# Query transposes a step ahead, and a new order of loads and TensorE work at the start, in a fused retention and feed-forward kernel

## The chip, the cores and the metric

The kernel runs on one core of a Trainium2 chip. The metric is the device time of one execution in microseconds (us). A profile is one further look at an execution; its span is some 2 us shorter than the device time, because the program's ends are not in it. All runs told of are of the fast state unless said otherwise. "Step" is the work on 256 tokens (there are twelve, 0 to 11); the steps 0 to 2 are written out ahead of the main loop, which runs from 3 to 11. At the undisturbed pace a step of the loop takes 12.18 us.

## The reference

```python
# retention: per head h a 64x64 state that decays by gamma[h] at every token
for t in range(S):                                    # S = 768, 4 batches, 8 heads, D = 64
    state = gamma * state + outer(k[:, :, t], v[:, :, t])
    y[:, :, t] = scale * q[:, :, t] @ state
x = y as rows of [B*S, H*D]                           # 3072 x 512
# feed-forward without activation
a = x @ w1; b = x @ w2                                # 512 -> 1024
out = (a * b) @ w3 @ w_out                            # w3 @ w_out is multiplied once, in the kernel
```

The kernel computes the recurrence in chunks of 64 tokens: scores of queries with keys inside a chunk, masked; their product with the scaled values ("attention" below); and a running state from keys and values, whose product with the queries is added. Queries and keys must be transposed for that. In the loop the DMA engine does it.

## The kernel before

Everything below is issued in program order on each engine: there is no scheduler between. All DMAs, loads, stores and transposes, are issued by SyncE, in this order. Cuts are marked.

```python
    w3_st = {f: load_rows(moe_w3, f) for f in range(4, 8)}
    load_q(0); load_q(1)
    load_k(0); load_v(0)
    w1_st = [load_rows(moe_w1, d) for d in range(4)]
    load_k(1); load_v(1)
    w2_st = [load_rows(moe_w2, d) for d in range(4)]
    # ... q2, q3, then keys, values and queries of the steps 2 to 4

    def q_dma(n):                 # transpose of one query tile, issued on SyncE
        qT = att.tile([128, 2, NP, 128], HP, tag="qT", name="qT", bufs=5)
        nc.sync.dma_start_transpose(qT..., q16s.pop(n)[:, :])       # cut

    def step(m):
        inter(m - 1)              # state products of the step before
        outputs_back(m - 1, 0); outputs_back(m - 1, 1)              # VectorE
        am_back = scores(m)       # needs the keys of m and BOTH query tiles of the pair
        am_back(0); am_back(1)
        if m > 5:
            q_dma(m + 2)
        ffn[m - 2].o_unit(0)      # 8 output products, eviction on ScalarE, store
        k_cast(m + 1, (nc.scalar,)); k_dma(m + 1)
        ffn[m - 2].o_unit(1)
        load_k(m + 2); load_v(m + 2)
        load_q(m + 3 if m < 6 else m + 4)
        for f in range(2):
            ffn[m - 1].ab(f)      # a- and b-products; ScalarE and VectorE evict
        if m == 5:
            q_cast(7, nc.scalar); q_dma(7); load_q(9)
        intra(m)                  # attention
        # ... kv, state updates, ab(2), ab(3)
        v_cast(m + 1, (nc.gpsimd, nc.gpsimd))
        if m == 4:
            q_cast(6, nc.gpsimd); q_dma(6)
        elif m > 4:
            q_cast(m + 3, nc.gpsimd)
        for f in range(4, 8):
            ffn[m - 1].ab(f)
```

Two query tiles serve two steps: 6 and 7 for the steps 6 and 7. Both are needed when step 6's scores begin.

Of the kernel before, what the change touches and what calls it, by code (L numbers as in the profile page):

```python
# [18 lines left out]
def kernel(  # L19
# [11 lines left out]
    nc = tc.nc  # L31
# [47 lines left out]
    def load_k(m):  # L79
        load_kv(m, k_in, k)  # L80

    def load_v(m):
        load_kv(m, v_in, v)
# [41 lines left out]
    w3_st = {f: load_rows(moe_w3, f) for f in range(4, 8)}  # L125
    load_q(0)
    load_q(1)
    load_k(0)
    load_v(0)
    w1_st = [load_rows(moe_w1, d) for d in range(4)]  # L130
    load_k(1)
    load_v(1)
    w2_st = [load_rows(moe_w2, d) for d in range(4)]
    load_q(2)
    load_q(3)
# [56 lines left out]
    def cast_to(dst, src, on_dve):  # L192
        if on_dve:
            nc.vector.tensor_copy(dst, src)
        else:
            nc.scalar.copy(dst, src)  # L196
# [78 lines left out]
    def k_cast(m, engs):  # L275
        k16 = att.tile([128, 2, 512], HP, tag="k16", name="k16", bufs=3)
        k32 = k_in.pop(m)
        if len(engs) == 1:
            parts = [(k16[:, :, :].rearrange("p e x -> p (e x)"), k32[:, :, :].rearrange("p e x -> p (e x)"))]
        else:  # L280
            parts = [(k16[:, e, :], k32[:, e, :]) for e in range(2)]
        for eng, (dst, src) in zip(engs, parts):
            (nc.scalar.copy if eng is nc.scalar else eng.tensor_copy)(dst, src)  # L283
        k16s[m] = k16

    def v_cast(m, engs):
        v16 = att.tile([128, 2, 512], HP, tag="v16", name="v16", bufs=3)
        v32 = v_in.pop(m)
        for e, eng in enumerate(engs):
            eng.tensor_tensor(  # L290
                v16[:, e, :].rearrange("j (h d) -> j h d", d=D),
                v32[:, e, :].rearrange("j (h d) -> j h d", d=D),
                VS[:, :].unsqueeze(2).broadcast_to((128, H, D)),
                MULT,
            )
        v16s[m] = v16
# [25 lines left out]
    def k_transposes(m, tag, on_dve):  # L322
        k16, kT = k16s[m], new_kT(m)
        if tag:
            ps = bank(tag, [128, 2, NP, 128], HP, "psTk")
        else:
            ps = ps_f.tile([128, 2, NP, 128], HP, tag="psF", name="psTk")
        for e in range(2):
            for p in range(NP):
                nc.tensor.transpose(ps[:, e, p, :], k16[:, e, p * 128 : (p + 1) * 128], ident16[:, :])  # L330
        for e in range(2):
            cast_to(kT[:, e, :, :], ps[:, e, :, :], on_dve[e])
# [17 lines left out]
    def scores(m, engs=None):  # L350
        kT = kTs.pop(m)
        am = att.tile([128, 2, NP * 2, L], HP, tag="am", name="am")
        ps = [bank(f"X{r}", [128, NP * 2, L], FP, "psA") for r in range(2)]
        for e in range(2):
            for p in range(NP):
                for r in range(2):
                    for s in range(2):
                        nc.tensor.matmul(  # L358
                            ps[r][half(s), p * 2 + e, :], lhsT=kT[half(r), e, p, half(s)],
                            rhs=queries(m, e, p, s, r), start=True, stop=True,  # L360
                        )
        AMs[m] = am

        def back(r):
            nc.vector.tensor_tensor(  # L365
                am[:, r, :, :], ps[r][:, :, :],
                keep[:, :].unsqueeze(1).broadcast_to((128, NP * 2, L)), MULT,
            )

        return back  # L370
# [52 lines left out]
    def inter(m):  # L423
        ps = psYs[m]
        t = [Ts[m, s] for s in range(2)]
        first = t[0] is None
        for e in range(2):
            for p in range(NP):
                u = p * 2 + e
                for s, r in ((1, 0), (1, 1)) if first else ((1, 0), (0, 1), (0, 0), (1, 1)):  # L430
                    nc.tensor.matmul(  # L431
                        ps[s][half(r), u, :], lhsT=t[s][half(r), u * L : (u + 1) * L],
                        rhs=queries(m, e, p, s, r), start=False, stop=(e == 1 and p == NP - 1),
                    )

    def outputs_back(m, s):
        if m not in XT:
            XT[m] = xpool.tile([128, NP * 2, 2, L], HP, tag="xt", name="xt")
        order = "p u (t i) -> p u t i"
        nc.vector.tensor_tensor(  # L440
            XT[m][:, :, s, :].rearrange("p u (i t) -> p u t i", t=2),
            psYs[m][s][:, :, :].rearrange(order, t=2),
            YS[:, :, :].rearrange("p a (e x) -> p (a e) x", e=2).rearrange(order, t=2), MULT,
        )
# [52 lines left out]
    def cast_w(W, st, d, on_dve):  # L497
        cast_to(W[d][:, :], st[d][:, :], on_dve)

    def busy(m, tag="Y0"):  # L500
        ps = bank(tag, [128, 512], FP, "psZ")
        for _ in range(m):
            nc.tensor.matmul(ps[:, :], lhsT=Z[:, 0:128], rhs=Z[:, 0:512], start=True, stop=True)  # L503
# [30 lines left out]
    k_transposes(0, "X0", (True, False))  # L534
    w3o_back()
    v_cast(0, (nc.gpsimd, nc.vector))
    nc.gpsimd.tensor_copy(W1[1][:, :], w1_st[1][:, :])
    cast_w(W1, w1_st, 0, False)
    backs = []

    def first_scores():
        backs.append(scores(0))

    w3o_back = w3_mm(7, first_scores)
    w3o_back()
    backs[0](0)
    backs[0](1)
    intra(0)
    backs.append(kv(0, True))
    busy(3, "X0")  # L550
    backs[1](0)
    inter(0)
    busy(3, "X1")
    outputs_back(0, 0)
    outputs_back(0, 1)
    backs[1](1)
    cast_w(W1, w1_st, 2, False)
    cast_w(W1, w1_st, 3, False)

    ffn = [Ffn(m) for m in range(NSTEP)]  # L560
    f0, f1 = ffn[0], ffn[1]
# [3 lines left out]
    def four_banks():  # L565
        return [ps_f.tile([128, 2, TB], FP, tag="psF", name="psF")[:, :, :] for _ in range(4)]

    def by_rows(W, ps, d, blocks=range(8)):
        for f in blocks:
            nc.tensor.matmul(  # L570
                ps[f // 2][:, f % 2, :], lhsT=W[d][:, f * 128 : (f + 1) * 128],
                rhs=f0.x(d), start=(d == 0 and f % 2 == 0), stop=(d == 3 and f % 2 == 1),
            )

    k_cast(1, (nc.gpsimd, nc.scalar))
    ps = four_banks()
    by_rows(W1, ps, 0)
    by_rows(W1, ps, 1)
    by_rows(W1, ps, 2)
    k_transposes(1, "Y0", (True, False))  # L580
    by_rows(W1, ps, 3, range(4))
    pa = [hold[i // 2][:, i % 2 * 512 : i % 2 * 512 + 512].rearrange("p (a n) -> p a n", a=2) for i in range(4)]
    am_back = scores(1)
    by_rows(W1, ps, 3, range(4, 8))
    for i in range(4):
        cast_to(pa[i], ps[i], False)
    am_back(0)
    am_back(1)
    v_cast(1, (nc.gpsimd, nc.gpsimd))
    nc.gpsimd.tensor_copy(W2[0][:, :], w2_st[0][:, :])  # L590
    ps = four_banks()
    cast_w(W2, w2_st, 1, False)
    intra(1)
    kv_back = kv(1)
    kv_back(0, nc.vector)
    by_rows(W2, ps, 0)
    inter(1)
    outputs_back(1, 1)
    outputs_back(1, 0)
    cast_w(W2, w2_st, 2, False)  # L600
    nc.gpsimd.tensor_copy(W2[3][:, 512:1024], w2_st[3][:, 512:1024])
    q_cast(2, nc.gpsimd)
    kv_back(1)
    by_rows(W2, ps, 1)
    nc.scalar.copy(W2[3][:, 0:512], w2_st[3][:, 0:512])
    by_rows(W2, ps, 2)
    f1.a_unit(0, "X0")
    by_rows(W2, ps, 3)
    for i in range(4):
        nc.vector.tensor_tensor(f0.HT[:, 2 * i : 2 * i + 2, :], pa[i], ps[i], MULT)  # L610
    q_cast(3, nc.gpsimd)
    for f, tag in ((1, "Y1"), (2, "Y0"), (3, "X1"), (4, "X0"), (5, "Y1"), (6, "Y0"), (7, "X1")):
        f1.a_unit(f, tag)
    k_cast(2, (nc.gpsimd, nc.scalar))
    q_transposes(2, "X0", True)
    f0.o_unit(0)
# [27 lines left out]
    def step(m):  # L644

        inter(m - 1)
        outputs_back(m - 1, 0)
        outputs_back(m - 1, 1)
        if m >= NSTEP:
            return  # L650
        am_back = scores(m)
        am_back(0)
        am_back(1)
        if m > 5:
            q_dma(m + 2)
        ffn[m - 2].o_unit(0)
        if m + 1 < NSTEP:
            k_cast(m + 1, (nc.scalar,))
            k_dma(m + 1)
        ffn[m - 2].o_unit(1)  # L660
        load_k(m + 2)
        load_v(m + 2)
        load_q(m + 3 if m < 6 else m + 4)
        for f in range(2):
            ffn[m - 1].ab(f)
        if m == 5:
            q_cast(7, nc.scalar)
            q_dma(7)
            load_q(9)
        intra(m)  # L670
        kv_back = kv(m)
        kv_back(0)
        ffn[m - 1].ab(2)
        ffn[m - 1].ab(3)
        kv_back(1)
        if m + 1 < NSTEP:
            v_cast(m + 1, (nc.gpsimd, nc.gpsimd))
        if m == 4:
            q_cast(6, nc.gpsimd)
            q_dma(6)  # L680
        elif m > 4:
            q_cast(m + 3, nc.gpsimd)
        for f in range(4, 8):
            ffn[m - 1].ab(f)
# [42 lines left out]
```

## Time and profile before

| | before |
|---|---|
| device time, median of 3 | 198.76 us (197.88 to 199.11) |
| span of the profile | 196.1 us |
| TensorE busy | 180.8 us, 92% |
| granted clock, mean | 0.983 |

The busy share reads as if TensorE were the bound everywhere. It is, in the steps; but one wait stands out in the list of what TensorE's matmuls waited for (total us, how often, the longest):

```profile
PE psA L358 <- DMA qT<-q: 5.2, 1, 5.2
```

One wait, once: 5.2 us for a query transpose. The next longest waits in that list are of 1.3 and 1.1 us, at the start of the program and at the second step's keys.

### The profile page before, as it was taken

The numbers are of one execution on the slowest core, as the hardware profiler recorded it, in microseconds if no ns is written. First come the engines' busy times: TensorE is split into PE (matmuls) and PEld (weight loads), VectorE is DVE, ScalarE is ACT, GpSimd is POOL, SyncE is SP. The second block draws the span as 40 slices with busy tenths as digits, with TensorE's granted clock in tenths as the row PEclk, the third lists the DMA queues.
The fourth block names the chain that finished last, engine by engine and source line by source line (L and its number), as shares of the span: only waits on it lengthen the run. The fifth ranks groups of instructions, "written<-read, shape, count | busy, mean of one in ns | idle before, by whom it ended". The sixth has DMA issues, their size and how long they took to land.

```text
span 196.1 us, 6231 instructions
## 1 busy us (share of the span) xinstructions
PE 180.8 (92%) x2651; PEld 126.8 (65%) x2651; DVE 96.7 (49%) x187; ACT 87.5 (45%) x165; POOL 64.1 (33%) x92
## 2 busy tenths in 40 slices
PE   7799998679998999999908999999999999999993
PEld 2355655558675785877803685877858678586772
DVE  1226356068378255674432265664556735555240
ACT  5578545475553544327400544325443264232432
POOL 6200233536618071280601044280732607120000
PEclk9999999999999999999995899999999999999999
DMA  6999999999999999999998696989969550110202
GB/s 213 370 390 384 255 278 344 270 357 250 231 220 238 253 205 234 226 244 215 258 229 154 166 233 162 243 206 187 207 162 215 116 160 3 57 53 3 107 0 107
DMA packets 87338, 40.23 MB, mean 205 GB/s; under 512 B 67728, under 2 KB 82320, under 8 KB 87312
## 3 DMA queue, kind: packets, MB, share of 16 engines
q1 hardware_dynamic: 87312, 39.85, 84.0%
q8 instruction: 20, 0.33, 0.7%
q14 instruction: 6, 0.05, 0.1%
HBM read 29.36 MB, written 6.29 MB: 182 GB/s over the span
## 4 chain that ended last, share of the span: by engine, by line
PE 68%; SPq 12%; DMA 11%; DVE 4%; ACT 1%; issue 1%; DVEq 0%; ACTq 0%
PE psF L460 33%; PE psO L485 23%; SPq L60 12%; DMA stg<-in_moe_w_out_dram 4%; DMA stg<-in_k_dram 4%; DMA qT<-q 3%; PE psY L431 3%; PE psA L358 2%; PE psG L460 2%; PE psY L380 2%; PE psF L570 1%; DVE ht L475 1%; PE psK L400 1%; DVE am L365 1%; PE psTk L330 1%
## 5 line engine op out<-in xcount | busy, mean ns | idle before, releaser
L460 PE MATMUL psF<-xt,w 128*128 128x256 f16 x672 | 77.1, 273 | 0.0
L460 PEld LDWEIGHTS <-w 128*128 128x128 f16 x704 | 68.0, 98 | 10.3
L475 DVE TENSOR_TENSOR ht<-pa,psF 128x256 f16<-128x256 f32 x88 | 36.6, 420 | 54.3 <-ACT pa L469 29.7
L418 POOL TENSOR_TENSOR t<-s,GS 128x512 f16<-128x512 f32 x19 | 24.1, 1267 | 71.8 <-DVE s L417 71.8
L469 ACT COPY pa<-psF 128x256 f32<-128x256 f32 x80 | 29.7, 371 | 39.9 <-PE psF L460 39.9
L485 PE MATMUL psO<-w3o,ht 128*128 128x512 f16 (+2 forms) x200 | 46.2, 386 | 0.0
L485 PEld LDWEIGHTS <-ht 128*128 128x128 f16 x200 | 19.2, 101 | 21.5 <-issue 3.3
L489 ACT ACTIVATE osb<-psO 128x512 f32<-128x512 f32 (+2 forms) x25 | 14.5, 580 | 40.0 <-PE psO L485 40.0
L290 POOL TENSOR_TENSOR v<-stg,VS 128x512 f16<-128x512 f32 x23 | 23.5, 1042 | 5.5 <-DMA stg<-in_v_dram 3.9
L365 DVE TENSOR_TENSOR am<-psA,keep 128x512 f16<-128x512 f32 x24 | 15.3, 679 | 7.0 <-PE psA L358 7.0
L440 DVE TENSOR_TENSOR xt<-psY,YS 128x512 f16<-128x512 f32 x24 | 16.1, 722 | 1.7 <-PE psY L431 0.8
L269 POOL CAST q<-stg 128x1024 f16<-128x1024 f32 x8 | 8.3, 1036 | 23.6 <-DMA stg<-in_q_dram 23.6
L417 DVE TENSOR_TENSOR s<-psK,t 128x512 f32<-128x512 f32 x20 | 13.8, 688 | 3.4 <-PE psK L400 2.7
L283 ACT CAST k<-stg 128x1024 f16<-128x1024 f32 (+1 forms) x12 | 11.2, 934 | 5.1 <-DMA stg<-in_k_dram 4.9
L358 PE MATMUL psA<-qT,kT 64*64 64x64 f16 x384 | 6.6, 197 | 6.6 <-DMA qT<-q 5.2
L215 DVE COPY w3t<-psW 128x1024 f16<-128x1024 f16 x8 | 5.4, 689 | 11.7 <-PE psW L223 9.2
L358 PEld LDWEIGHTS <-kT 64*64 64x64 f16 x384 | 5.1, 108 | 8.1 <-issue 5.9
L196 ACT CAST w3h<-stg 128x1024 f16<-128x1024 f32 x8 | 8.3, 1043 | 3.6 <-DMA stg<-in_moe_w_dram 3.5
L431 PEld LDWEIGHTS <-t 64*64 64x64 f16 x352 | 6.5, 109 | 3.6 <-issue 2.1
L503 PE MATMUL psZ<-zeros 128*128 128x512 f16 x19 | 7.6, 553 | 1.3 <-DVE zeros L142 1.3
L431 PE MATMUL psY<-qT,t 64*64 64x64 f16 x352 | 7.8, 194 | 0.7 <-DVE t L418 0.6
L244 PE MATMUL psW<-wo,w3t 128*128 128x512 f16 x32 | 8.4, 399 | 0.0
(58 smaller groups left out, 121.2 us busy)
## 6 DMA issues: line engine op xcount, KB each, us to landing
stg<-in_moe_w_dram SPq DMA_DIRECT2D x16, 512.0 KB, 6.6
stg<-in_q_dram SPq DMA_DIRECT2D x12, 512.0 KB, 6.9
stg<-in_k_dram SPq DMA_DIRECT2D x24, 256.0 KB, 5.4
stg<-in_v_dram SPq DMA_DIRECT2D x24, 256.0 KB, 5.2
out_dram<-osb SPq DMA_DIRECT2D x23, 256.0 KB, 2.5
stg<-in_moe_w_out_dram SPq DMA_DIRECT2D x4, 512.0 KB, 7.8
out_dram<-osb SPq DMA_DIRECT2D x1, 160.0 KB, 1.8
qT<-q SPq DMA_TRANSPOSE x8, 4.0
```

The source lines that it names most:

```text
L60: nc.sync.dma_start(dst, src)
L290: eng.tensor_tensor(v16[:, e, :].rearrange("j (h d) -> j h d", d=D), v32[:, e, :].rearrange("j (h d) -> j h d", d=D), VS[:, :].unsqueeze(2 ...
L358: nc.tensor.matmul(ps[r][half(s), p * 2 + e, :], lhsT=kT[half(r), e, p, half(s)], rhs=queries(m, e, p, s, r), start=True, stop=True,)
L365: nc.vector.tensor_tensor(am[:, r, :, :], ps[r][:, :, :], keep[:, :].unsqueeze(1).broadcast_to((128, NP * 2, L)), MULT,)
L418: eng.tensor_tensor(t16[:, :], s32[:, :], gs, MULT)
L431: nc.tensor.matmul(ps[s][half(r), u, :], lhsT=t[s][half(r), u * L : (u + 1) * L], rhs=queries(m, e, p, s, r), start=False, stop=(e == 1 an ...
L440: nc.vector.tensor_tensor(XT[m][:, :, s, :].rearrange("p u (i t) -> p u t i", t=2), psYs[m][s][:, :, :].rearrange(order, t=2), YS[:, :, :] ...
L460: nc.tensor.matmul(ps[:, :], lhsT=W[d][:, f * 128 : (f + 1) * 128], rhs=self.x(d), start=(d == 0), stop=(d == 3),)
L469: nc.scalar.copy(self.pa[f][:, :], ps[:, :])
L475: nc.vector.tensor_tensor(self.HT[:, f, :], self.pa.pop(f)[:, :], ps[:, :], MULT)
L485: nc.tensor.matmul(psO[:, :], lhsT=self.HT[:, f, e * 128 : (e + 1) * 128], rhs=W3O[f][:, cs], start=(f == 0), stop=(f == 7),)
L489: nc.scalar.activation(osb[:, cs], psO[:, :], AF.Copy, scale=final_scale)
```

## The change

Its intent: (1) take the late query transpose out of the loop's way, by casting both tiles of a pair in one place and issuing both transposes at the head of the step before they are needed (query 7 is cast at the end of step 4 instead of in the middle of step 5; query 6's transpose moves from the end of step 4 to the head of step 5); (2) in the start-up, load the second step's keys and values ahead of w1, compute its attention early, and have the a-products of the second step fill the time in which w2's rows come in.

```diff
     load_q(1)
-    load_k(0)
-    load_v(0)
+    for m in range(2):
+        load_k(m)
+        load_v(m)
     w1_st = [load_rows(moe_w1, d) for d in range(4)]
-    load_k(1)
-    load_v(1)
     w2_st = [load_rows(moe_w2, d) for d in range(4)]
@@ start-up, attention of step 0
-    nc.gpsimd.tensor_copy(W1[1][:, :], w1_st[1][:, :])
-    cast_w(W1, w1_st, 0, False)
+    k_cast(1, (nc.gpsimd, nc.scalar))
     ...
     backs.append(kv(0, True))
-    busy(3, "X0")                      # filler matmuls
     backs[1](0)
+    k_transposes(1, "X0", (False, False))
+    w3o_back()
     inter(0)
-    busy(3, "X1")
     outputs_back(0, 0)
     outputs_back(0, 1)
     backs[1](1)                        # state update, GpSimd
-    cast_w(W1, w1_st, 2, False)
-    cast_w(W1, w1_st, 3, False)
+    v_cast(1, (nc.gpsimd, nc.gpsimd))  # values of step 1, GpSimd
+    nc.gpsimd.tensor_copy(W1[1][:, :], w1_st[1][:, :])
+    for d in (0, 2, 3):
+        cast_w(W1, w1_st, d, False)
@@ attention of step 1, W1's and W2's rows (before: W1's rows, keys, scores, W2's rows and attention in turn)
+    busy(2, "X1")
     am_back = scores(1)
     am_back(0)
     am_back(1)
     intra(1)
     kv_back = kv(1)
     kv_back(0, nc.vector)
+    by_rows(W1, ps, 0)
     inter(1)
     ...
+    by_rows(W1, ps, 1)  ...  by_rows(W1, ps, 3)
+    f1.a_unit(f, tag)                  # f = 0..3
     by_rows(W2, ps, 0)
+    f1.a_unit(f, tag)                  # f = 4..7
     by_rows(W2, ps, 1)  ...  by_rows(W2, ps, 3)
-    f1.a_unit(f, tag)                  # f = 1..7, after w2's last row
@@ loop
-        if m > 5:
+        if m > 3 and m % 2:
+            q_dma(m + 1)
             q_dma(m + 2)
     ...
+        load_q(m + 3) if m % 2 == 0 else None
         load_k(m + 2)
         load_v(m + 2)
-        load_q(m + 3 if m < 6 else m + 4)
+        load_q(m + 3) if m % 2 else None
     ...
-        if m == 5:
-            q_cast(7, nc.scalar)
-            q_dma(7)
-            load_q(9)
     ...
-        if m == 4:
-            q_cast(6, nc.gpsimd)
-            q_dma(6)
-        elif m > 4:
+        if m % 2 == 0:
+            q_cast(m + 2, nc.gpsimd)
             q_cast(m + 3, nc.gpsimd)
```

(The second and third blocks are cut to their core and partly put in order for reading; the loop's are whole.)

More of the change, by code (lines that the diff above doesn't have):

```diff
@@ L544 @@
     w3o_back = w3_mm(7, first_scores)
-    w3o_back()
     backs[0](0)
@@ L573, in by_rows @@
             )
-    k_cast(1, (nc.gpsimd, nc.scalar))
-    ps = four_banks()
-    by_rows(W1, ps, 0)
-    by_rows(W1, ps, 1)
-    by_rows(W1, ps, 2)
-    k_transposes(1, "Y0", (True, False))
-    by_rows(W1, ps, 3, range(4))
     pa = [hold[i // 2][:, i % 2 * 512 : i % 2 * 512 + 512].rearrange("p (a n) -> p a n", a=2) for i in range(4)]
+    busy(2, "X1")
     am_back = scores(1)
-    by_rows(W1, ps, 3, range(4, 8))
-    for i in range(4):
-        cast_to(pa[i], ps[i], False)
     am_back(0)
     am_back(1)
-    v_cast(1, (nc.gpsimd, nc.gpsimd))
-    nc.gpsimd.tensor_copy(W2[0][:, :], w2_st[0][:, :])
-    ps = four_banks()
-    cast_w(W2, w2_st, 1, False)
     intra(1)
@@ L595 @@
     kv_back(0, nc.vector)
-    by_rows(W2, ps, 0)
+    ps = four_banks()
+    by_rows(W1, ps, 0)
     inter(1)
@@ L599 @@
     outputs_back(1, 0)
+    by_rows(W1, ps, 1)
+    kv_back(1)
+    nc.gpsimd.tensor_copy(W2[0][:, :], w2_st[0][:, :])
+    by_rows(W1, ps, 2)
+    by_rows(W1, ps, 3)
+    for i in range(4):
+        cast_to(pa[i], ps[i], i % 2 == 1)
+    cast_w(W2, w2_st, 1, False)
+    for f, tag in ((0, "X0"), (1, "Y1"), (2, "Y0"), (3, "X1")):
+        f1.a_unit(f, tag)
+    ps = four_banks()
+    by_rows(W2, ps, 0)
     cast_w(W2, w2_st, 2, False)
+    for f, tag in ((4, "X0"), (5, "Y1"), (6, "Y0"), (7, "X1")):
+        f1.a_unit(f, tag)
+    by_rows(W2, ps, 1)
+    nc.scalar.copy(W2[3][:, 0:512], w2_st[3][:, 0:512])
     nc.gpsimd.tensor_copy(W2[3][:, 512:1024], w2_st[3][:, 512:1024])
     q_cast(2, nc.gpsimd)
-    kv_back(1)
-    by_rows(W2, ps, 1)
-    nc.scalar.copy(W2[3][:, 0:512], w2_st[3][:, 0:512])
     by_rows(W2, ps, 2)
-    f1.a_unit(0, "X0")
     by_rows(W2, ps, 3)
@@ L611 @@
     q_cast(3, nc.gpsimd)
-    for f, tag in ((1, "Y1"), (2, "Y0"), (3, "X1"), (4, "X0"), (5, "Y1"), (6, "Y0"), (7, "X1")):
-        f1.a_unit(f, tag)
     k_cast(2, (nc.gpsimd, nc.scalar))
```

## The prediction

> **What bounds the kernel now.** I read the page's busy shares first, then the slices of TensorE, its clock and the DMA, then the chain of waits, then TensorE's waits, and last the timeline where the chain leaves TensorE.
>
> ```profile
> span 196.1 us, 6231 instructions
> PE 180.8 (92%) x2651; PEld 126.8 (65%) x2651; DVE 96.7 (49%) x187; ACT 87.5 (45%) x165; POOL 64.1 (33%) x92
> ...
> PE   7799998679998999999908999999999999999993
> ...
> PEclk9999999999999999999995899999999999999999
> DMA  6999999999999999999998696989969550110202
> ```
>
> TensorE is busy 92% of the span, no other engine half of it. Its row has two weak places: slices 7 to 9 (about 34 to 49 us, the start-up) and a zero at slice 20 (98 to 103 us), directly followed by the only two slices with a low clock. The DMA row is full to about 98 us, so the start-up is fed at the rate of the loads.
>
> The chain of waits, in order of time, around that zero:
>
> ```profile
> 97.19 1.02 SPq L60
> 98.21 0.05 issue
> 98.26 0.02 SPq L313
> 98.28 0.03 issue
> 98.31 5.24 DMA qT<-q
> 103.54 0.04 issue
> 103.59 0.43 PE psA L358 x12
> 104.02 6.03 PE psO L485 x16
> 110.05 1.75 PE psF L460 x16
> ```
>
> The scores of step 6 wait for a transpose of queries. It could only be issued at 98.31, because SyncE issues in order and was busy up to then with the loads of step 5. It lands 5.24 us later. The 16 output products after it take 6.03 us; in every other step the same entry reads 3.56. TensorE's clock, stretch by stretch:
>
> ```profile
> 98.00:100.00 2.00, 0.43 (x36) 0.34 (x29) 1.53 (x3) 0.00 (x0) 0.00 (x0) 1.00 0.82 182
> 100.00:102.00 2.00, 0.00 (x0) 0.00 (x0) 0.00 (x0) 0.00 (x0) 0.00 (x0) 1.00 1.18 280
> 102.00:103.00 1.00, 0.00 (x0) 0.00 (x0) 0.00 (x0) 0.00 (x0) 0.25 (x1) 0.58 1.09 223
> 103.00:104.00 1.00, 0.41 (x17) 0.35 (x17) 0.00 (x0) 0.00 (x0) 0.79 (x1) 0.50 1.15 294
> ```
>
> (After the bounds and length stand the busy times of PE, PEld, DVE, ACT and POOL, then granted clock, DMA share, GB/s.) After some 4 us of idleness the clock falls to a half; it stays there to about 109 us.
>
> In the start-up the chain runs through a load, the second step's keys:
>
> ```profile
> 28.07 8.59 DMA stg<-in_k_dram
> 36.66 0.02 issue
> 36.68 0.63 ACT k L283
> 37.31 0.05 issue
> 37.35 0.41 PE psTk L330 x4
> ```
>
> **What the Trainium skill says.** (1) "TensorE: Matmul & The Clock Gate", section "Why this matters for your kernels": keep TensorE's idle gaps under about 3 us, or one idle window puts it back to half clock. The trace agrees: 5.2 us of idleness cost the clock, the start-up's gaps (longest 1.1 us in the waits) did not. (2) "Perfetto Trace Analysis", section "DMA Instruction — HWDGE (DVE, Sync)": the profiled span of a DMA instruction is the issuing sequencer's part; the data movement is not in it. Here too: that transpose has a span of 2.36 us on SyncE but lands 5.24 us after its start. (3) "DMA: Bandwidth & Descriptors", section "Why small descriptors are slow (HBM only)": a 256-byte descriptor carries a fixed overhead. The keys and values are such rows (64 floats). The trace agrees: the casts that wait for loads start at 30.05, 31.33, 32.58 and 34.00 for the four w1 rows of 512 KB (1.3 us apart), then 35.18 and 36.68 for two halves of the keys of 256 KB (1.5 us apart), so about half the rate.
>
> **Part 1: query transposes a step ahead.** Now the transpose for query 7 is issued in the middle of step 5, behind five loads; after the change both casts (queries 6 and 7) run on GpSimd at the end of step 4, and both transposes head the SyncE queue of step 5, ahead of its stores, key transpose and loads. Nothing is added: as many transposes as before, and one query cast moves from ScalarE to GpSimd (1.04 us each on either). GpSimd has room: it is busy 4.5 us of the 12.18 us of step 4.
>
> What it takes away: from the start of step 5's outputs (86.33) to that of step 7's (118.30) the kernel needs 31.97 us, and two undisturbed steps need 2 × 12.18 = 24.36. Excess: 7.6 us, of which 5.2 are the wait and 2.5 the half clock (6.03 − 3.56). All of it lies on the path.
>
> Is the new place early enough? GpSimd finishes the values of step 5 at 86.56 and casts query 6 by 87.55, as before. Query 7's load now goes ahead of keys and values in step 4, so issue near 81 to 82, and with the 6.9 us that such loads take it has landed by 89; cast by 90. SyncE: transpose 6 at 87.57 (2.48 us), transpose 7 at about 90.05 (1.2 to 2.5 us), a store, then the key transpose of step 6 at about 92.5 to 93.2 instead of 90.78. Key transposes land 3.0 to 5.7 us after issue, median 3.4: 96 to 98.5. Needed at 98.1. So it is just in time; I charge 0.5 us. The loads of step 6 and 7's keys slip by about 2.5 us with it, but keys are cast on ScalarE some 9 us before their scores. In later steps the DMA share falls (0.84 in the step from 118.30), so the pairs of transposes cost nothing there.
>
> **Part 2: the start-up.** The bytes up to w2's end are the same, so w2's last row still lands at 44.3. Only the order changes. I shift landings by the gaps seen: keys 1 at about 29.7 and 31.0, values 1 at 32.3 and 33.4, w1's rows at 35.0, 36.3, 37.6, 38.9. Filler matmuls fall from 6 to 2: 4 × 0.27 = 1.1 us of TensorE work less.
>
> TensorE then, with durations from the timeline: transposes of keys 1 end near 32.1 (the ScalarE half waits for the load), the first step's state products near 32.55, filler, scores of step 1 at 33.5 to 33.95 (after two ScalarE evictions of 0.58). Next it needs step 1's scaled values. They stand on GpSimd behind the state update, which waits for VectorE's outputs (32.4 to 33.75) and sum (0.69): update 34.5 to 35.75 (1.27), values 36.8 and 37.8 (2 × 1.04). So TensorE is nearly idle from 33.95 to 37.8, but for 0.2 us at 36.9. Then: 0.8 us of attention, W1's first row, 0.6 us waiting for the state, W1's other rows (0.87 each) to 43.25. Here f1's a-products (8 × 0.436 = 3.5) and W2's rows (4 × 0.87 = 3.5) follow almost without gaps, with ScalarE nearly full (four casts or halves, eight copies of 0.37, two evictions): W2's last row ends near 50.7, not 46.6, but with the a-products done. Two query transposes, the key transpose and both outputs, partly behind four VectorE products of 0.69: scores of step 2 near 55.9, against 54.51. So a loss of 1.3 us. Of it about 0.4 comes back at step 3's keys: before, TensorE waited 0.38 us for that cast. Net +0.9: the a-products come forward in the order, but the hole in front of step 1's attention, 3.9 us, is larger than the idleness that they fill. Since orders like this are usually tuned on a chip and my landing times may be off by a microsecond, I count +0.6, and add 0.3 for the chance (one in eight) that the hole costs the clock for some 2.5 us.
>
> **Sum.** 198.76 − 7.6 + 0.5 + 0.9 = 192.56, say 192.6 us (ratio 0.969).
>
> **The rivals.** (a) *The wait moves to the key transpose.* SyncE stays in order and now has three transposes in a row in step 5. For it: transposes and loads in the stretch 86 to 98 us run at a DMA share of 1.20, and the chain of waits before 98 us is already all SyncE. Against it: 0 to 2 us of slack by the sum above. If it is late by 2 us (no clock loss), the time is 194.1. (b) *The start-up gains.* If keys land earlier or GpSimd keeps values ahead, the a-products before w2 save up to the 3.1 us that they take after w2's last row now: 189 us. Against it: TensorE's work is the same but for 1.1 us, and step 3's keys were cast at 57.86 only on landing, with the DMA full, so it can't run far ahead. (c) *The hole before step 1's attention costs the clock.* Idle 3.9 us with a blip of 0.2, close to the 4 us after which it fell at 102; then some 2.5 us more: 195. (d) *The DMA loses its pause.* In the wait it caught up; without it, step 6's keys and values may be late. Against it: a steady step from 118.30 moves 193 GB/s, and 233 to 236 were moved in steps 4 and 5.
>
> **Range and chances.** The wait's removal is sure to about 0.7 us as far as it goes; (a) takes up to 2, the start-up lies between −2.5 and +3. Low 189.5, high 195.8. The limit for 2% is 194.8; (a) and (c) together or a bad start-up reach it: faster 0.81, within 2% 0.17, slower 0.02.
>
> **What would show it.** Right: TensorE's row without a zero and its clock without a low slice after 98 us; steps 5 and 6 of 12.2 us; no wait for a query transpose over 0.5 us; both transposes issued between 87 and 93 us. Start-up: a gap of TensorE of 3 to 4 us at about 34 to 38, ended by GpSimd's values; step 2's scores at about 56. Wrong: a wait of scores for a key transpose of over 1 us in step 6; a half clock at 38 to 44; or step 2's scores before 54, which would mean that the landing times or GpSimd's order were misjudged.

## The result, and the profile after

| | before | after |
|---|---|---|
| device time, median of fast runs | 198.76 us (3 runs) | 192.12 us (191.48 to 193.78, 4 runs) |
| ratio | | 0.9687, interval 0.9598 to 0.9777: faster |
| span of the profile | 196.1 us | 192.1 us |

Ratios here are the mean time of one kernel's fast runs over that of the other's of the same rounds, as the record gives them, so not quite the ratio of the medians. Redone from the single times, some of them leave out a profiled execution; that moves them by 0.001 or less, but for the one told of in experiment 10. A later run of the kernel before in the changed kernel's rounds took 202.87 us and is left out as slow. The profiled execution after the change was its slowest, 193.78 us, and that of before one of its fastest, 197.82: two spans alone would understate the gain. The result is correct in all runs told of here.

The page after the change, the lines that answer to those of before:

```profile
span 192.1 us, 6226 instructions
PE 179.4 (93%) x2647; PEld 126.9 (66%) x2647; DVE 97.4 (51%) x188; ACT 84.7 (44%) x163; POOL 65.0 (34%) x93
...
PE   7799988299999799999999998999999999999993
...
PEclk9999999859999999999999999999999999999999
DMA  5999999999999799999999998999989960110202
```

Two readings. The zero at slice 20 is gone, and so is the low clock behind it. But there is a new low place: slice 7 of TensorE, 34 to 38 us, is down to 2, and in this slice and the next the clock is at 8 and 5 tenths. The chain of waits through the loop, where the stall was (start, duration, what):

```profile
100.47 0.56 PE psY L430 x28
101.08 0.27 PE psA L357 x26
101.36 3.56 PE psO L484 x16
```

Step 6's scores follow at once on step 5's state products, and its 16 output products take 3.56 us, where before stood a wait of 5.24 and products of 6.03. A few lines further down the same chain has something that was not in the kernel before:

```profile
109.61 7.66 DMA stg<-in_k_dram
...
118.29 0.60 ACT osb L488
118.93 0.60 PE psF L459 x4
```

Keys for step 8 take 7.66 us from their issue to landing; ScalarE waits for them with an output's eviction queued behind; the matmuls, out of free accumulators, wait 0.8 us for this eviction. The same chain (keys, ScalarE, eviction, matmuls) stands there once more at 142 us, with hardly any wait of the matmuls.

The new hole in the start-up, on TensorE's timeline (start, duration, instruction, and in brackets the idle time before it and who ended it):

```profile
33.35 0.56 PE L357 MATMUL psA<-qT,kT 64*64 64x64 f16 x32
36.61 0.33 PE L379 MATMUL psY<-am,v 64*64 64x64 f16 x16 [2.70 <-POOL v L289]
37.61 0.43 PE L379 MATMUL psY<-am,v 64*64 64x64 f16 x16 [0.67 <-POOL v L289]
...
38.40 1.89 PE L569 MATMUL psF<-xt,w 128*128 128x256 f16 x8
```

and GpSimd's at the same time:

```profile
34.30 1.26 POOL L417 TENSOR_TENSOR t<-s,GS 128x512 f16<-128x512 f32 x1 [3.70 <-DVE s L416]
35.52 2.04 POOL L289 TENSOR_TENSOR v<-stg,VS 128x512 f16<-128x512 f32 x2
```

The eight matmuls of W1's first row take 1.89 us; at full clock they take 1.05 (experiment 3). What they waited for are step 1's values, which GpSimd scales only after the state update.

To compare starts I use two marks in each profile's chain and timeline, which are free of how fast the very first loads came: the first scores (step 0) and the first of step 3's output products; and as a third the first output products behind the loop.

| profile | first scores | outputs of step 3 | first outputs behind the loop | start-up part | loop part |
|---|---|---|---|---|---|
| before | 28.37 | 62.04 | 179.09 | 33.67 | 117.05 |
| after | 28.84 | 64.82 | 175.06 | 35.98 | 110.24 |

So in this pair the loop gained 6.81 us, the start-up lost 2.31, and the first scores came 0.47 later: 4.0 us together, the difference of the spans. These are one profile each; further profiles below show that the start-up part of one and the same order varies by up to 2 us between profiles.

### The profile page after: what moved, and what is told of

It is laid out like the page before. It is cut to its first block, busy times and chain, and to the rows that moved or that the text cites. A ratio compares the mean times of both kernels' runs of the same rounds, so it can differ in the third digit from the quotient of the medians.

```text
span 192.1 us, 6226 instructions
## 1 busy us (share of the span) xinstructions
PE 179.4 (93%) x2647; PEld 126.9 (66%) x2647; DVE 97.4 (51%) x188; ACT 84.7 (44%) x163; POOL 65.0 (34%) x93
## 4 chain that ended last, share of the span: by engine, by line
PE 65%; DMA 15%; SPq 11%; issue 4%; POOL 2%; ACT 2%; DVE 0%; ACTq 0%; DVEq 0%; POOLq 0%
PE psF L459 32%; PE psO L484 19%; DMA stg<-in_k_dram 10%; SPq L60 9%; PE psF L569 5%; DMA stg<-in_moe_w_out_dram 4%; PE psY L430 3%; PE psG L459 2%; PE psY L379 2%; PE psA L357 1%; PE psK L399 1%; POOL v L289 1%; SPq L489 1%; ACT osb L488 1%; POOL t L417 1%
## 5 line engine op out<-in xcount | busy, mean ns | idle before, releaser
L459 PE MATMUL psF<-xt,w 128*128 128x256 f16 x672 | 77.4, 273 | 0.8 <-ACT osb L488 0.8
L484 PE MATMUL psO<-w3o,ht 128*128 128x512 f16 (+2 forms) x200 | 44.1, 371 | 0.0
L484 PEld LDWEIGHTS <-ht 128*128 128x128 f16 x200 | 18.3, 98 | 20.3 <-DVE ht L609 1.4
L268 POOL CAST q<-stg 128x1024 f16<-128x1024 f32 x9 | 9.2, 1041 | 17.3 <-DMA stg<-in_q_dram 17.3
L569 PE MATMUL psF<-xt,w 128*128 128x256 f16 x64 | 9.7, 317 | 0.0
L379 PE MATMUL psY<-am,v 64*64 64x64 f16 x384 | 5.8, 197 | 3.8 <-POOL v L289 3.4
L379 PEld LDWEIGHTS <-v 64*64 64x64 f16 x384 | 4.4, 110 | 6.6 <-POOL v L289 3.6
```

The source lines that it names most:

```text
L459: nc.tensor.matmul(ps[:, :], lhsT=W[d][:, f * 128 : (f + 1) * 128], rhs=self.x(d), start=(d == 0), stop=(d == 3),)
L484: nc.tensor.matmul(psO[:, :], lhsT=self.HT[:, f, e * 128 : (e + 1) * 128], rhs=W3O[f][:, cs], start=(f == 0), stop=(f == 7),)
L569: nc.tensor.matmul(ps[f // 2][:, f % 2, :], lhsT=W[d][:, f * 128 : (f + 1) * 128], rhs=f0.x(d), start=(d == 0 and f % 2 == 0), stop=(d == ...
```

## The experiments

### 1 and 2. Each part alone

`q_ahead_only` is the kernel before with the loop of the changed one, and nothing else of it; `startup_only` is the changed kernel with the loop of the one before. Their edits are the blocks of the diff above, from "loop" on or up to it.

> The kernel before with the query part of the change alone (casts and transposes of queries a step ahead, load order of queries in the loop); the start-up stays as it was. Theory A (the query part brings all of the gain, the start-up part costs 2.8 us): no wait for a query transpose and no low clock at 98 to 109 us, 190 to 191.5 us, so faster than the whole change (192.1); step 2's scores at 54.5 us as before; 0.5 to 2 us may come back as late keys, for TensorE reaches the loop 2.8 us sooner at the same loads. Rival B (the start-up part helps too, its late end in the one profiled run is chance): slower than the whole change, 193 us or more.

Measured: 191.60 us, ratio 0.9641 (0.9580 to 0.9702), so at least as fast as the whole change. Start-up part 34.20 us, loop part 109.16 (63.70 to 172.86): 7.89 us less than before. Its clock row, from its page:

```profile
PEclk9999999999999999999999999999999999999999
```

> The kernel before with the start-up part of the change alone (keys and values of step 1 ahead of w1, new order); the query transposes stay as they were. Theory A: step 2's scores near 57.4 us instead of 54.5 and a half clock at about 37 to 43 us; the wait in step 6 stays, perhaps some 1 us shorter, because the loop starts later against the same loads; 200 to 202 us. Rival B: under 198 us, and no half clock in the start-up.

Measured: 199.22 us, ratio 1.001 (0.9966 to 1.0055): the same time as before. That is less than theory A's 200 to 202, and more than rival B's 198. Its profile has both losses:

```profile
PEclk9999999879999999999995899999999999999999
```

The clock is low once in the start-up (slices 7 and 8) and once behind the wait in step 6, which stands as it stood:

```profile
100.62 5.14 DMA qT<-q
...
105.81 0.43 PE psA L357 x11
```

Start-up part 34.76 us, 1.1 us longer than before; loop part 116.55, half a microsecond shorter. What follows: the query part brings all of the gain. (It changes the casts, the place of issue and the order of the query loads together; no run takes these apart.) The start-up part brings none, and its order does cost a hole and the clock, but the time it costs is smaller than theory A took from the first pair of profiles.

### 3. Filler matmuls in the hole

```diff
     am_back(0)
     am_back(1)
+    busy(12)
     intra(1)
```

> The kernel after with 12 filler matmuls (12 x 0.216 = 2.6 us) on TensorE between step 1's scores and its attention, where it idles for 2.7 us waiting for GpSimd's values. If the half clock from 37 to 43 us comes from that idleness: clock full throughout, the state products and W1's rows at their usual durations, start-up 2 to 3 us shorter, 189.5 to 190.5 us. If the low clock has another cause (or the hole alone, not the clock, costs the time): 191.5 to 193 us, clock still low there.

Measured: 192.42 us, ratio 0.9668 (0.9617 to 0.9720). The cause of the low clock is confirmed, the price is not. The granted clock was 1.0 in all four executions, against 0.980 to 0.991 in the ten timed runs of the unedited change, here and in later rounds. W1's first row was back at 1.05 us. The fillers delay nothing: step 1's attention begins 7.77 us after the first scores in both profiles. The start-up part was 34.03 us, against 35.98 in the change's first profile and 34.81 in its second (below). But the mean of the timed runs is 192.26 us, with the unedited change at 192.38 in other rounds: a full clock in the start-up was worth nothing that these runs can resolve, where 2 to 3 us were expected. The time expectation failed.

### 4. The values first on GpSimd

```diff
-    backs[1](1)
     v_cast(1, (nc.gpsimd, nc.gpsimd))
+    backs[1](1)
```

> The kernel after with GpSimd's two value products of step 1 moved ahead of its state update of step 0 (1.26 us), which nothing needs before 38 us. Theory A (the hole is GpSimd's order): the wait for values falls from 3.4 us to under 1.5, TensorE starts step 1's attention at about 35 instead of 36.6, the clock stays full, step 2's scores come at 53.5 to 55 instead of 57.4, time 188.5 to 190. Rival C (the values' landing, not GpSimd, is what ends the hole): GpSimd waits for the loads instead, the hole stays over 2.5 us, time 191.5 or more.

Measured: 191.28 us, ratio 0.9621 (0.9565 to 0.9677). The hole is GpSimd's order, not the values' landing: GpSimd starts them at 32.40, and TensorE's attention of step 1 begins at 34.82, held by VectorE's masks, no longer by the values:

```profile
32.40 2.04 POOL L289 TENSOR_TENSOR v<-stg,VS 128x512 f16<-128x512 f32 x2 [1.82 <-DVE t L413]
...
34.82 0.19 PE L379 MATMUL psY<-am,v 64*64 64x64 f16 x1 [0.96 <-DVE am L364]
```

Step 2's scores come at 53.94 (57.30 in the unedited change's profile, 54.51 before): the start-up part is 32.67 us, the shortest so far. Yet 191.28 us lies above the 188.5 to 190 that I expected, and the clock stayed full in the profiled execution only (0.998): the other three had 0.989, 0.980 and 0.981. The profile shows a further loss, in the loop: its steps 3 and 4 took 12.85 and 12.49 us instead of 12.18. Its chain in step 4:

```profile
73.06 4.58 DMA stg<-in_k_dram
...
78.69 0.60 ACT osb L488
79.33 0.60 PE psF L459 x4
```

Keys hold ScalarE, an eviction waits behind them, the matmuls wait for the eviction. My reading is that the loads are further behind the sooner TensorE arrives in the loop; that is argued. The loop part is 110.13 us, one microsecond over the shortest.

### 5 and 6. The change and its query part once more, in the same rounds

> The changed kernel, unedited, so that it stands in the same rounds as the query part alone. Theory A': the start-up part costs 0.4 us for its order and 0.7 to 2 us for the half clock, which comes in every run but ends sooner or later; so 0.5 to 2 us slower than the query part alone, ratio to before 0.966 to 0.972. Rival B': the start-up part is neutral in the timed runs and the two profiles' difference is the loads' chance: within 0.5 us of it. In its profile: half clock from about 37 us; scores of step 0 to outputs of step 3 34.5 to 36 us.

> The query part alone once more. Theory A': 190.5 to 191.5 us, ratio 0.960 to 0.965, clock full or nearly so, scores of step 0 to outputs of step 3 33.5 to 34.3 us as in the kernel before. Rival B': ratio equal to that of the unedited change within 0.003.

Measured: the change 192.17 us, ratio 0.9662 (0.9606 to 0.9717); the query part alone 191.52 us, ratio 0.9618 (0.9566 to 0.9671). Means of six runs each: 192.39 and 191.73. Earlier, each in its own rounds, the means were 192.38 and 191.71. So the start-up part costs about 0.7 us of the whole, twice by the same amount, which is inside what theory A' forecast (0.5 to 2 us), though the intervals of the ratios overlap; it is not settled that it costs anything, but a gain is unlikely. Nor was the query part's clock full throughout: it was 0.982 to 1.0 in these six runs. The second profile of the change has a start-up part of 34.81 us and a loop part of 109.16, without the late keys' stalls of TensorE; the second profile of the query part 34.24 and 109.93, with one of 0.7 us. So late keys come in some executions of either kernel and not in others.

### 7. The clock behind the wait

To weigh the clock alone, the kernel before gets filler matmuls in the place where it waits:

```diff
+        if m == 6:
+            busy(24, "X0")
         am_back = scores(m)
```

> The kernel before with 24 filler matmuls (24 x 0.216 = 5.2 us) on TensorE ahead of step 6's scores, where it waits 5.2 us for the query transpose. If the 6.03 us of the outputs after the wait come from a clock lost to idleness: clock full there, outputs at 3.56 us, the wait itself unchanged, so 2.0 to 2.5 us faster than before (ratio 0.988 to 0.990). If they have another cause (the DMA's catching up, the evictions): outputs still over 5 us, ratio 0.997 to 1.003.

Measured: 197.51 us, ratio 0.9908 (0.9857 to 0.9960); the means of the fast runs are 197.51 and 199.31 (nine of the 11 runs of the kernel before; two are slow): about 1.8 us, with an interval of some 0.8 to 2.9, just under the forecast. The chain at the same place:

```profile
100.47 5.94 DMA qT<-q
...
106.45 0.32 PE psA L358 x16
106.77 3.56 PE psO L485 x16
```

The outputs behind the transpose take 3.56 us again, 2.47 less than before. The transpose is no earlier: in this profile it takes 5.94 us to land instead of 5.24, so that 0.7 us of the gain is lost again. So of what the query part removes, about 2 us were the clock that the wait cost, and the rest the wait. This run taught something else. Its start-up is that of the kernel before, and its clock row reads

```profile
PEclk9999999958999999999999999999999999999999
```

The low slices are 8 and 9, 39 to 49 us: the old start-up loses the clock too, in some executions. In this kernel's six runs the mean clock was 0.982 or 0.983 three times, 0.991 once and 1.0 twice; in the 11 runs of the unedited kernel before in these rounds it lay between 0.966 and 0.991.

### 8. Three more edits on top of the values first

```diff
     by_rows(W1, ps, 0)
+    by_rows(W1, ps, 1)
     inter(1)
     ...
-    by_rows(W1, ps, 1)
@@ step 2
-        k_transposes(3, None, (True, False))
+        k_transposes(3, None, (False, False))
@@ loads
+    load_k(5)                 # after the loads of step 4, before the loop
-        load_k(m + 2)
+        load_k(m + 3)
```

> The changed kernel with the values first on GpSimd and three further edits: W1's second row ahead of step 1's state products (TensorE waited 1.0 us there), both evictions of step 3's transposed keys on ScalarE (scores waited 1.1 us behind VectorE's queue), and each step's keys loaded one step earlier (late keys cost 0.8 to 1.0 us in two profiles). Expected: scores of step 0 to outputs of step 3 about 31 us (32.7 with the values first alone), first to last outputs of the loop 109.1 us, no wait for keys; 188.5 to 190 us, ratio 0.950 to 0.956. If the loads bound the start-up by then: 31.5 us or more there, 190 to 191 us; if the extra early keys push other loads late: a wait for values or a query transpose in steps 3 to 5.

Measured: 192.75 us, ratio 0.9686 (0.9625 to 0.9746): a failure, by its mean 1.8 us slower than the values first alone (193.08 and 191.32, of different rounds; the intervals of the ratios overlap). Start-up part 34.45, loop part 111.37. The clock was at 0.982 in five of six runs, at 0.991 in one. And the list of what TensorE's matmuls waited for has a new entry:

```profile
PE psA L358 <- DMA kT<-k: 2.0, 1, 2.0
```

Step 4's scores wait 2.0 us for their transposed keys. In the program's order the added load of step 5's keys stands in SyncE's queue ahead of the transposes for step 4: the key transpose is issued 9.6 us after the start of step 3's outputs, against 7.7 with the values first alone. I take this for the cause, which no run isolates. This is the third alternative that I had written down, at another transfer than I named. As three edits went in together, the run doesn't say what each of them did. Nor does it show that they lost the clock: the values first alone had 0.980 to 0.989 in three of four runs.

### 9 and 10. Fillers with the values first, and the keys' cast behind the evictions

```diff
     am_back(0)
     am_back(1)
+    busy(4)
     intra(1)
     ...
     by_rows(W1, ps, 0)
+    busy(4, "X0")
     inter(1)
```

> The changed kernel with the values first on GpSimd and 4 + 4 filler matmuls (0.216 us each) in the two places where TensorE still idled about 1 us each in that run: before step 1's attention and before its state products. If the start-up's granted clock is what spreads the values-first runs (188.6 us of span at 0.998, 190.7 at 0.981): clock 0.99 to 1.0 in nearly all runs, spans 188.5 to 189.3 us, time 190.2 to 191.0 us, ratio 0.952 to 0.957, faster than the query part alone (ratios 0.962 and 0.964). If the loads bound the steps after it whatever the start-up does: ratio 0.960 or more although the clock is full.

Measured: median 191.02 us and mean 191.03 of five fast runs (a sixth of 194.63 is slow), ratio 0.9578 (0.9533 to 0.9623), between the two forecasts. This is the lowest ratio of all kernels here. It was not run in the same rounds as the query part alone (191.72 on average over ten runs), so how much it is ahead of that is not settled. The clock was full, or nearly so (0.998), in every run. Start-up part 32.50 us; loop part 111.61. In the loop (60 to 190 us) its waits show where the head start went:

```profile
ACT k L282 <- DMA stg<-in_k_dram: 3.5, 2, 1.9
PE psF L459 <- ACT osb L488: 2.2, 2, 1.2
```

`warm_keys_after` adds to it:

```diff
-        if m + 1 < NSTEP:
-            k_cast(m + 1, (nc.scalar,))
-            k_dma(m + 1)
         ffn[m - 2].o_unit(1)
+        if m + 1 < NSTEP:
+            k_cast(m + 1, (nc.scalar,))
+            k_dma(m + 1)
```

> The same, and in each step ScalarE casts the next keys after both output evictions instead of between them, so that keys that come late from memory hold up no eviction (0.2 to 0.8 us of TensorE's waits in three profiles). If late keys cost the loop 0.7 to 1.1 us by that order: first to last outputs of the loop 109.1 us, no wait of matmuls for an output eviction, 0.3 to 0.8 us faster than the kernel without it. If the key transpose, which goes out about 1.5 us later then, is what binds: a wait of scores for a key transpose of 0.5 us or more, no gain or slower.

Measured: median 191.44 us and mean 191.31 of five fast runs (a sixth of 193.61 is slow): no gain. The ratio on record, 0.9626 (0.9581 to 0.9671), counts the slow run, as far as its value can be worked out, and leaves out the fast profiled one; the means of the fast runs (199.43 for the kernel before) give 0.959. The profile is as theory had it, loop part 109.60 us, no matmul waiting for an output's eviction, 0.3 us for a key transpose; span 188.4. The timed runs don't confirm a profile's one look.

All profiles in one table (us; the loop's shortest is 109.08):

| kernel | start-up part | loop part | sum |
|---|---|---|---|
| before | 33.67 | 117.05 | 150.72 |
| start-up part alone | 34.76 | 116.55 | 151.31 |
| change | 35.98 / 34.81 | 110.24 / 109.16 | 146.22 / 143.97 |
| query part alone | 34.20 / 34.24 | 109.16 / 109.93 | 143.36 / 144.17 |
| change, hole filled | 34.03 | 109.08 | 143.11 |
| values first | 32.67 | 110.13 | 142.80 |
| values first, fillers | 32.50 | 111.61 | 144.11 |
| the same, keys after | 33.03 | 109.60 | 142.63 |
| three more edits (8) | 34.45 | 111.37 | 145.82 |
| before, wait filled (7) | 35.65 | 115.21 | 150.86 |

The old start-up took 33.67, 34.20 and 34.24 us, and 35.65 in the profile in which it lost the clock; the new one, unedited, 34.76, 34.81 and 35.98. The means differ by 0.7 us, as the timed runs do; much of the 2.31 us of the first pair seems to be the chance of single executions.

Among the kernels that have the query part, start-up parts differ by 3.5 us. The two shortest are followed by loops of 111.6 and 110.1 us. The medians of the fast runs lie within 191.0 and 192.4 (192.8 with the three edits of experiment 8). A start-up that is faster by a microsecond or two can be partly lost again when loads are late in the first steps of the loop; the waits quoted show this at work in two profiles, though not that it explains the whole spread.

## Why the prediction was right

It said 192.6 us (189.5 to 195.8) and a ratio of 0.969; measured were 192.12 and 0.9687, later 192.17 and 0.9662. By its steps:

- **The wait and the clock, 7.6 us.** Right, and by the named split. The query part alone made the loop 7.9 us shorter in its first profile and 7.1 in its second. The clock's share, which I had put at 2.5 us, measured about 1.8 us with the wait left in place and filled, in an interval that holds 2.5.
- **Just in time, 0.5 us charged for the key transpose of step 6.** The order held: in the profile after, both query transposes are issued from 90.35 to 94.82 and the key transpose at 95.57, with step 6's scores at about 101. As step 5 began 2.8 us later there (outputs at 89.19, against 86.41), this is the order and the distance that I had forecast. No scores waited for keys there. But the half microsecond went elsewhere. I had written that pairs of transposes in later steps cost nothing because the DMA has room. In one of two profiles keys came late in the steps 7 and 9: from step 6's outputs to step 8's and on to step 10's it took 25.04 and 24.58 us, where the query part alone took 24.18 and 24.37, so 0.9 and 0.2 us. Rival (d), the DMA without its pause, is not shown to be the cause. The DMA share (the column before the last) is indeed higher than in the kernel before, which had 0.96, 0.97 and 0.80 in these stretches. But it is higher still in the second profile of the change (the lower three lines), in which no matmul waited for late keys:

```profile
110.00:122.00 12.00, 11.21 (x187) 8.06 (x185) 6.25 (x13) 4.53 (x10) 6.17 (x6) 1.00 1.06 215
122.00:134.00 12.00, 12.00 (x209) 8.95 (x207) 7.07 (x14) 4.92 (x11) 4.35 (x5) 1.00 1.16 203
134.00:146.00 12.00, 11.95 (x207) 8.76 (x205) 6.82 (x14) 4.71 (x11) 6.10 (x7) 1.00 1.03 230
...
110.00:122.00 12.00, 12.00 (x195) 8.92 (x193) 6.71 (x15) 5.03 (x12) 6.61 (x7) 1.00 1.19 195
122.00:134.00 12.00, 12.00 (x208) 8.96 (x206) 7.22 (x15) 4.98 (x11) 4.31 (x5) 1.00 1.19 258
134.00:146.00 12.00, 12.00 (x209) 8.94 (x208) 6.94 (x14) 5.00 (x11) 6.30 (x7) 1.00 1.19 199
```

  Both profiles issue the keys for step 8 equally soon (7.25 and 7.19 us after the start of step 6's outputs). What differs is how long they take to land, and why stays open.
- **The start-up, +0.9 us.** The hole was forecast at 33.95 to 37.8 us, with a blip at 36.9, ended by GpSimd's values; it was there from 33.9 to 37.6, with its blip at 36.61, and by the values. Its cost to the clock was misjudged: I gave it one chance in eight, and it came in both profiles and, by the mean clock, in all ten timed runs. The half clock, from 36.8 to 43.6 us in the first profile, is one of the signs of being wrong that I had written down myself. I had also read the old start-up as safe from it, from one profile; experiment 7 shows otherwise. Step 2's scores came at 57.30 and 55.95 (forecast 55.9). By the means of the profiles the start-up loses 0.7 us, and by the timed comparison with the query part alone about 0.7 us of the end time, near the 0.9 of the sum. That the term came out near its size is partly luck: the clock was lost always instead of seldom, and the loss cost less than the 2.5 us that I had put on it.
- **Rivals.** (a), the wait moving to the key transpose, did not come. (b), a start-up that gains 3 us, did not come either; its kernel of truth is the order of GpSimd, which made the start-up shorter than before once it was turned (experiment 4). (c), the clock lost to the hole, came; experiment 3, which takes the clock loss away, shows none of the 2.5 us of end time that I had attached to it.

Open is why a full clock in the start-up (experiment 3) gains nothing measurable in the timed runs, although it shortens the start-up in the profile, by 0.8 to 2.0 us; and what each edit of experiment 8 did.

## What to carry to other kernels

Look in the chain of waits for a single long wait on an in-order queue before any share of busy time: here a transfer queued behind five loads cost 5.2 us and then about 2 more through the clock, in a kernel that was 92% busy. When two orders of a start-up are compared, give an engine's long job that nobody needs yet (here the state update) the later place in that engine's queue; in experiment 4 this shortened the start-up part, while the gain in time, 1.1 us of mean, is within the intervals. And judge a start-up by the end time: where the steps after it wait for loads, a microsecond saved early can be gone a few steps later.

## What the Trainium skill lacked or had wrong

- "TensorE: Matmul & The Clock Gate", section "Why this matters for your kernels", asks for idle gaps of no more than about 3 us. Here shorter ones cost the clock. In the two profiles of the change it fell to a half at about 36.8 and 37.8 us: in the first within 0.2 us of the end of a gap of 2.70 us, in the second after another gap of 0.68. In experiment 7 it fell in the start-up at about 39.2 us, where TensorE's longest gap since 34 us was 0.90. The kernel before with about the same gaps there (1.1 us at most) kept its clock in its profile, so the length of the single gap doesn't decide; what does, no run isolates.
- The same page, section "What's actually happening", gives a free-running window of 3413 ns. This fits the traces: the half clock behind the wait in the kernel before lasts from about 102.2 to 109.0 us, two such windows. It fits the mean clocks too: most timed runs lie near 1.0, 0.991, 0.983, 0.974 and 0.966, steps of some 0.0085, and half of 3.41 us in a span of 196 us is 0.0087 (an estimate from the page's figure). The page does not say that the mean clock of a run thus counts the lost windows; it is a handy reading.
- "Perfetto Trace Analysis", section "What "DMA-bound" means", names engines, sequencer and SBUF as what can bind. It lacks the case seen here, a load that is late for an in-order engine and thereby holds that engine's other work: in experiment 9 ScalarE's cast of keys, waiting 1.9 us, held an eviction for which the matmuls waited 1.2 us.
- No page says how much of a saving made early is lost again in a stage that waits for loads. Here 2.3 to 3.5 us (start-up parts of 34.81 and 35.98 us in the change, 32.50 in experiment 9, from single profiles) became 1.4 us of mean time (192.39 and 191.03, of different rounds).
